# Retuned rules for which product TensorE takes next in a fused adaLN + attention + mixer-MLP kernel

## The chip, the cores and the metric

The kernel runs on one core of one Trainium2 chip. The metric is the device time of one execution in microseconds (us); the reported value is the median of three runs. TensorE (PE in the profile, with its weight loads as PEld), VectorE (DVE), ScalarE (ACT), GpSimd (POOL) and SyncE (SP, which issues the DMAs) run side by side and meet at semaphores.

## The reference

`x` is 2048 x 512. Six modulation rows come from `silu(c) @ w_mod`. Then, with layer norms that are scaled and shifted by these rows:

```python
h = _layernorm(x) * (1 + ca) + sa
x = x + ga * attention(h, wqkv, wo)              # 32 heads of 16
h = _layernorm(x) * (1 + cb) + sb
# mixer block B
g  = _gelu(_layernorm(h) @ w1)                   # its 4 column groups shifted by +1, -1, +2, -2 rows
x1 = h + shifted(g) @ w2
x  = x + gb * (x1 + _gelu(_layernorm(x1) @ w3) @ w4)   # 512 -> 1792 -> 512
```

In the attention each head forms `softmax(q k^T / 4) v` over 2048 keys.

## The kernel before, in words

**Work.** Heads are taken in pairs (16 pairs) and queries in four chunks of 512: 64 units. A unit has 16 key tiles of 128 keys. For each key tile and head TensorE makes one score product `sc` (line 1036, 64 rows of the array, 512 columns). ScalarE turns it into exponentials (line 1032), stored as 32-bit words. The upper 16 bits of each word are used as they are; GpSimd scales the lower 16 bits (`p_low`, line 1087), or ScalarE does it in two halves when GpSimd is far behind. To know the row maxima beforehand TensorE also makes, 24 key tiles ahead (`LEAD`), the maximum product `mb` (line 1020), and VectorE reduces it (line 1016). One `mb` for one head and one `sc` for the other use the two halves of the array at the same time; the text calls the two a *row pair*. There are 2048 `mb` and 2048 `sc`. The *P·V products* `pv` come in groups of four that share the array by columns: a group with the upper halves of one key tile (line 1113), a group with the lower halves of two key tiles (line 1110), the *late* one. All else is *other products*: the q, k and v projections, wo, w1 to w4 (each as three products of split factors, lines 355, 357 and 359; `w1` to `w4` and `wo` read their weights from the tile `wr`), and transposes (`ot`, `xT`, `tr`).

**PSUM.** Seven banks are shared by `mb`, `sc` and the other products, which may hold up to three; the eighth holds `pv`. A row pair needs two free banks: one that VectorE has reduced and one that ScalarE has read.

**Order.** Nothing is decided on the chip. A planner in Python (`Sched` and the loop at the end of the kernel function) writes the instructions in one fixed order, with a clock of its own for each engine. It calls a run of products of one kind a *lump* and remembers the kind in `mode`: `"r"` (rows), `"c"` (P·V), `"o"` (other). `Sched.to` adds `SWITCH` to TensorE's planned clock at each change of kind and `ENTER` besides where the new kind is not P·V.

In each turn the loop finds `nc_`, the number of P·V groups that are ready (at most `CMOST` = 6), and `slack`, the time until the banks and the reading engine would let a lump of `GRP` = 3 row pairs run without a wait. Inside a lump of fewer than three pairs a next pair is called if its wait is at most `STAY`. From another kind a row lump is called when `slack` is at most `BACK` = 150 ns, unless there is so much *credit* (owed time of other products, filled at each row by `budget`) that it passes `CHIGH`. If no row is called, P·V runs when `CMIN` = 4 groups are ready (or fewer that fit into the slack); else other products run, while the clock is below `now + slack + GRACE` and credit is above zero, or above `-OVER` while a product sits half done in its bank (`sch.open`). If none of these ran, a row is called once its first pair has banks.

Of the kernel before, what the change touches and what calls it, by code (L numbers as in the profile page):

```python
# [50 lines left out]
OVER = 3000.0  # L51
CROW, CCOL, CIN, CMID, COUT = 232.0, 230.0, 105.0, 95.0, 95.0
# [28 lines left out]
VP = 2  # L81
UWAIT = 4
XB = 4
SWITCH, ENTER = 95.0, 107.0
EARLY, STAY, BACK, GRACE = 300.0, 300.0, 150.0, 0.0
OWE, CTOP, OMIN = 1500.0, 7000.0, 0.0
CHIGH, CMIN, CMOST, PTLOW, PLAG = 6500.0, 4, 6, 2, 1


class Sched:  # L90

# [235 lines left out]
def kernel(ctx, tc, A_x, A_wqkv, A_wo, B_w1, B_w2, B_w3, B_w4, c, w_mod, out):  # L327
# [83 lines left out]
    sch = Sched()  # L411
# [509 lines left out]
    def drain(flag):  # L921
        while flag not in done:
            sch.step()
# [50 lines left out]
    pts = [at.tile([P, 2, CH], I32, name=f"pt{i}") for i in range(NPT)]  # L974
# [97 lines left out]
    def p_low(s):  # L1072

        p = pt[s].rearrange("p j n -> p (j n)")
        o, i = p.bitcast(F16)[:, 0::2], p.bitcast(U16)[:, 0::2]
        ready = e_exp.pop(s) + XX
        g, a = [max(sch.T[e], ready) for e in "GA"]
        if g > a + LACT:

            def half(h):  # L1080
                c = slice(h * CH, (h + 1) * CH)
                e_low[s] = XP["A"] + sch.crit("A", 690, ready, partial(act.activation, o[:, c], i[:, c], AF.Copy, scale=0.5))
            half(0)
            e_low[s] += 690 + 480
            second.append(partial(half, 1))
        else:
            e_low[s] = XP["G"] + sch.crit("G", 1345, ready, lambda: pool.tensor_scalar(  # L1087
                o, i, 0.5, 1.0, op0=OP.mult, op1=OP.mult))
# [38 lines left out]
    def ac_copy():  # L1127
        u, e = acs.pop()
        if u:
            drain(("of", u - 1))  # L1130
        ac = at.tile([P, CH], F32, name="ac", tag="ac", bufs=1)
        acc = pv.pop(u)
        e = sch.crit("A", cA(), e + PX, lambda: act.activation(ac, acc, AF.Copy))
        v_free[0] = e + XP["A"]
        sch.add(o_fin(u, ac, e + XP["A"]), 0)
# [439 lines left out]
    def budget(s):  # L1575
        if s < 0:
            return 800.0
        return min(BTOP, max([BLOW] + [(1000.0 * w - sch.spent) / (d - s) for d, w in DUES if d > s]))
# [5 lines left out]
    def before(s):  # L1584

        nu, r = divmod(s + 32, 16)
        if r == 0 and 0 < nu < NU:
            asked.append(nu)
        if asked:
            ci, pr = units[asked[0]]  # L1590
            keys = [("kq", pr // 4)] + [("q", pr // 8)] * (ci > 0)
            if r >= UWAIT:
                for key in keys:
                    drain(key)
            if all(key in done for key in keys):
                load_unit(asked.pop())
        if s in VAT:
            i = VAT.index(s)
            for kt in range(4 * i, 4 * i + 4):
                while kt not in near and ("vk", 0, kt) not in done:  # L1600
                    sch.step()
                if kt not in near:
                    sch.dma(dma.dma_start, vst[i][:, kt % 4], Vs[0, :, kt])
        if s == NS - 12:
            done.add("keys")
        if s == -12:
            unit_tiles(at, 2, dve, pool)
# [18 lines left out]
    def cols():  # L1626
        n, t = 0, sch.T["P"] + (sch.mode != "c") * SWITCH
        for y in pvs[:CMOST]:
            if n and y[0] % NKT == 0 and not y[1]:
                break  # L1630
            if col_at(y) > t + 20:
                break
            t += CCOL
            n += 1
        return n

    def fillers():
        for e in "ADG":
            sch.misc(e, max(sch.T["P"], sch.T[e]) + TOLE[e])

    def do_cols(n):
        sch.to("c")
        for y in pvs[:n]:
            if not y[1]:
                e_hi.pop(y[0])
            pv_part(*y)
        del pvs[:n]

    def do_row(x, t):
        sch.T["P"] = t  # L1650
        sch.to("r")
        late = sorted(e_exp)
        one_row(x)
        for q in late:
            if 2 * q < x - 2 * PLAG:
                p_low(q)
# [3 lines left out]
    while x < end or pvs or acs:  # L1660
        if acs:
            ac_copy()
        can = x < end
        if can:
            s, i = divmod(x, 2)
            if x == LENDS:
                sch.most = MOST
            if i == 0 and seen != s:
                seen = s
                before(s)  # L1670
                if s >= 0 and s % 16 == 0:
                    drain(("shift", s // 16))
            can = i or s < 0 or bool(pts)
        now, row, slack = sch.T["P"], False, LATE
        if can:
            need = (s >= 0) + (s + LEAD < NS)
            sch.flush(need)
            free = sorted(sm.t)
            one = free[need - 1 + 2 * (s < 0)]
            if one >= LATE:  # L1680
                one = free[need - 1]
            enter = (sch.mode != "r") * (SWITCH + ENTER)
        else:
            for q in sorted(e_exp):
                p_low(q)
            while second:
                second.pop(0)()
        nc_ = cols()
        if can:
            if sch.mode == "r" and burst < GRP:  # L1690
                slack = one - now
                row = slack <= STAY
            else:
                st = one
                for k in range(2, GRP + 1):
                    if need * k <= len(free) and free[need * k - 1] < LATE:
                        st = max(st, free[need * k - 1] - (k - 1) * CROW)
                dry = sch.T["D"] if s + LEAD < NS else sch.T["A"]
                slack = max(st, dry - CROW - PX - EARLY) - enter - now
                row = slack <= BACK and (sch.mode == "r" or sch.credit < CHIGH and not (nc_ >= CMIN and len(pts) <= PTLOW))  # L1700
        if not row:
            n = 0
            if nc_ >= CMIN or nc_ and slack >= nc_ * CCOL + (sch.mode != "c") * SWITCH:
                do_cols(nc_)
                n = nc_
            elif slack >= OMIN or sch.mode == "o" or sch.credit > CHIGH:
                stop = now + max(slack, 0.0) + GRACE
                while (sch.T["P"] < stop or sch.credit > CHIGH) and sch.credit > (-OVER if sch.open else 0.0) and sch.one():
                    n += 1
            if not n:  # L1710
                if not can or one - enter > now + 100.0:
                    sch.T["P"] = now + 50.0
                else:
                    row = True
        if row:
            do_row(x, max(now, one - enter))
            burst = 1 if enter else burst + 1
            x += 1
            sch.credit = max(min(sch.credit + budget(s) / 2, CTOP), -OWE)
        fillers()  # L1720
        if tp[0] is None and x >= 2 * (NS // NC + TPO) and (x >= 2 * (NS // NC + TPL) or all(key in done for key in KEYS)):
            for key in KEYS:
                drain(key)
            qpx.close()
            tpx = ExitStack()
            tp[0] = tpx.enter_context(tc.tile_pool(name="tp", bufs=1, side="right"))
# [43 lines left out]
```

## Time and profile before

| what | value |
|---|---|
| median of 3 runs | 2010.18 us (2007.87 to 2010.95) |
| the profiled execution's own time | 2012.32 us |
| its span, first to last instruction | 2010.5 us |
| granted TensorE clock, mean | 0.99 |
| instructions | 42313 |
| HBM read, written | 225.81 MB, 62.91 MB |

The profile was taken from one execution whose own time is 2.1 us above the median. A timeline row gives the start, the length, the engine, the line, the operation with the tile written and the tiles read, the shapes and a count. Matmuls are pipelined, so the length of one (0.39 to 0.5 us) says less than the distance between two starts, and the text goes by starts.

### The profile page before, as it was taken

The numbers are of one execution on the slowest core, as the hardware profiler recorded it, in microseconds if no ns is written. First come the engines' busy times: TensorE is split into PE (matmuls) and PEld (weight loads), VectorE is DVE, ScalarE is ACT, GpSimd is POOL, SyncE is SP. The second block draws the span as 40 slices with busy tenths as digits, with TensorE's granted clock in tenths as the row PEclk, the third lists the DMA queues.
The fourth block names the chain that finished last, engine by engine and source line by source line (L and its number), as shares of the span: only waits on it lengthen the run. The fifth ranks groups of instructions, "written<-read, shape, count | busy, mean of one in ns | idle before, by whom it ended". The sixth has DMA issues, their size and how long they took to land.

```text
span 2010.5 us, 42313 instructions
## 1 busy us (share of the span) xinstructions
PE 1960.9 (98%) x14480; PEld 1131.9 (56%) x14480; DVE 1681.5 (84%) x3010; ACT 1483.1 (74%) x3087; POOL 1672.8 (83%) x1598
## 2 busy tenths in 40 slices
PE   6999999999999999999999999999999999999899
PEld 4655565555445555555455555555555655555798
DVE  7978878888988898888999889888988888883643
ACT  5377798878878777777887877787787877777343
POOL 6378889999988898888899989898899989887532
PEclk8999999999999999999999999999999999999999
DMA  5677588776533333335333334333433343333432
GB/s 184 195 208 232 170 247 274 229 250 212 200 97 105 114 114 126 122 109 166 104 105 114 105 111 126 126 113 110 156 110 96 118 135 114 114 94 128 158 149 90
DMA packets 233083, 293.24 MB, mean 146 GB/s; under 512 B 125876, under 2 KB 178052, under 8 KB 216580
## 3 DMA queue, kind: packets, MB, share of 16 engines
q1 hardware_dynamic: 232868, 290.53, 45.4%
q8 instruction: 115, 1.88, 0.4%
q14 instruction: 100, 0.82, 0.1%
HBM read 225.81 MB, written 62.91 MB: 144 GB/s over the span
## 4 chain that ended last, share of the span: by engine, by line
PE 79%; DVE 10%; ACT 4%; DMA 2%; POOL 2%; issue 1%; SPq 1%; POOLq 0%; ACTq 0%; DVEq 0%
PE mb L1020 15%; PE sc L1036 13%; PE pv L1113 11%; PE w L355 8%; PE w L357 8%; PE w L359 7%; PE pv L1110 7%; DVE mx L1016 6%; ACT pt L1032 2%; PE ot L1145 1%; POOL pt L1087 1%; PE xT L1223 1%; PE v L355 1%; PE mr L660 1%; PE v L359 1%
## 5 line engine op out<-in xcount | busy, mean ns | idle before, releaser
L1016 DVE TENSOR_REDUCE mx<-mb 128x1 f32<-128x512 f32 x2048 | 1296.5, 683 | 139.8 <-PE mb L1020 112.8
L1087 POOL TENSOR_SCALAR pt<-pt 128x1024 f16<-128x1024 uint16 x977 | 1301.2, 1366 | 103.7 <-ACT pt L1032 99.9
L1032 ACT ACTIVATE pt<-sc 128x512 int32<-128x512 f32 x2048 | 1100.1, 602 | 313.6 <-PE mb L1020 238.5
L1020 PE MATMUL mb<-kst,qtl 64*128 64x512 f32 x2048 | 732.5, 449 | 15.2 <-DVE mx L1016 4.1
L1036 PE MATMUL sc<-qtl,kst 64*128 64x512 f32 x2048 | 705.7, 441 | 4.4 <-DVE mx L1016 2.2
L1020 PEld LDWEIGHTS mb<-kst,qtl 64*128 64x128 f32 x2048 | 342.8, 193 | 183.1 <-DVE mx L1016 80.2
L1036 PEld LDWEIGHTS sc<-qtl,kst 64*128 64x128 f32 x2048 | 333.4, 185 | 129.3 <-issue 45.7
L1113 PE MATMUL pv<-pt,vst 128*32 128x512 f16 x4096 | 359.0, 394 | 2.2 <-DMA vst<-Vs 2.1
L1110 PE MATMUL pv<-pt,vst 128*17 128x512 f16 (+1 forms) x2048 | 213.8, 399 | 0.5 <-POOL pt L1087 0.3
L1447 POOL TENSOR_TENSOR g<-xs,g 128x256 fp32r<-128x256 f32 (+2 forms) x144 | 103.4, 719 | 96.1 <-ACT g L1446 92.4
L1113 PEld LDWEIGHTS <-vst 128*32 128x32 bf16 x4096 | 114.4, 94 | 119.2 <-issue 69.9
L355 PE MATMUL w<-A,wr 128*128 128x256 f32 (+2 forms) x576 | 174.9, 304 | 0.7 <-ACT A L349 0.5
L357 PE MATMUL w<-A,wr 128*128 128x256 f32 (+2 forms) x576 | 172.9, 300 | 0.5 <-DVE A L345 0.3
L359 PE MATMUL w<-A,wr 128*128 128x256 f32 (+2 forms) x576 | 172.9, 300 | 0.0
L1110 PEld LDWEIGHTS <-vst 128*17 128x17 f16 (+1 forms) x2048 | 54.0, 90 | 139.5 <-issue 130.1
L355 PEld LDWEIGHTS w<-A,wr 128*128 128x128 f32 x576 | 110.3, 191 | 28.1 <-issue 19.5
L357 PEld LDWEIGHTS w<-A,wr 128*128 128x128 f32 x576 | 110.1, 191 | 24.6 <-issue 23.3
L359 PEld LDWEIGHTS w<-A,wr 128*128 128x128 f32 x576 | 110.1, 191 | 24.4 <-issue 24.4
L355 PE MATMUL w<-wr,g 128*128 128x512 f32 x288 | 122.6, 426 | 0.6 <-ACT g L1446 0.6
L357 PE MATMUL w<-wr,g 128*128 128x512 f32 x288 | 119.5, 415 | 0.0
L359 PE MATMUL w<-wr,g 128*128 128x512 f32 x288 | 119.2, 414 | 0.2 <-POOL g L1447 0.2
L1437 DVE SCALAR_TENSOR_TENSOR sq<-sq,w 128x256 f32<-128x256 f32 (+2 forms) x144 | 60.4, 420 | 47.0 <-ACT sq L1443 44.2
(150 smaller groups left out, 2099.4 us busy)
## 6 DMA issues: line engine op xcount, KB each, us to landing
wr<-Ws SPq DMA_DIRECT2D x80, 1024.0 KB
kst<-Ks SPq DMA_DIRECT2D x189, 256.0 KB
vst<-Vs SPq DMA_DIRECT2D x252, 192.0 KB
qtl<-Qs SPq DMA_DIRECT2D x192, 64.0 KB
Vs<-vt SPq DMA_DIRECT2D x32, 384.0 KB
Ws<-wq SPq DMA_DIRECT2D x40, 256.0 KB
Ws<-wst SPq DMA_DIRECT2D x40, 256.0 KB
wst<-in_B_w_dram SPq DMA_DIRECT2D x36, 256.0 KB
```

The source lines that it names most:

```text
L355: te.matmul(o, lh, rh, start=first, stop=False)
L357: te.matmul(o, lh, rl, start=False, stop=False)
L359: te.matmul(o, ll, rh, start=False, stop=last)
L1016: end = sch.crit("D", 605, e + PX, lambda: dve.reduce_max(mxs[u][:, j, g, c:c + 1], b, axis=AX.X))
L1020: return ready, lambda: te.matmul(b, lhs, kst[u % 3][r, c * CH:(c + 1) * CH], start=True, stop=True), after
L1032: ea = sch.crit("A", 480, e + PX, lambda: act.activation(pt[s][:, j], b, AF.Exp))
L1036: return ready, lambda: te.matmul(b, kst[u % 3][r, kt * P:(kt + 1) * P], qst[u][r], start=True, stop=True), after
L1087: e_low[s] = XP["G"] + sch.crit("G", 1345, ready, lambda: pool.tensor_scalar(o, i, 0.5, 1.0, op0=OP.mult, op1=OP.mult))
L1110: te.matmul(acc[r:r + n, :], v[:, (kt + i) % 4, c - n:c].bitcast(F16), pt[s + i].bitcast(F16)[:, j, 0::2], start=False, stop=kt == NKT - 2 ...
L1113: te.matmul(acc[r:r + 32, :], v[:, kt % 4, r:r + 32], pt[s].bitcast(F16)[:, j, 1::2], start=kt == 0, stop=False, skip_group_check=True)
L1437: dve.scalar_tensor_tensor(sq, sq, 1.0 / GELU_A, b, op0=OP.add, op1=OP.mult)
L1447: ("G", cG(n), lambda: pool.tensor_tensor(lo, xs, hi, op=OP.subtract)), (None, 0, end), bank=b)
```

## The change

It changes numbers of the planner and two of its conditions. `SWITCH` becomes 105. `STAY` becomes 200, `GRACE` 400, `CHIGH` 9000, `PTLOW` 3, `OVER` 1500. When P·V is the present kind, other products are begun only if the slack is at least `OMINC` = 800 ns. After rows, with credit above `OFIRST` = 1500 and more than `PTLOW` free buffers of exponentials, ready P·V groups are passed over for other products, unless they fit into the slack. No instruction's form changes.

```diff
-SWITCH, ENTER = 95.0, 107.0
+SWITCH, ENTER = 105.0, 107.0
 EARLY, STAY, BACK, GRACE = 300.0, 300.0, 150.0, 0.0
-OWE, CTOP, OMIN = 1500.0, 7000.0, 0.0
+OWE, CTOP, OMIN, OMINC, OFIRST = 1500.0, 7000.0, 0.0, 800.0, 1500.0
 CHIGH, CMIN, CMOST, PTLOW, PLAG = 6500.0, 4, 6, 2, 1
+CHIGH = 9000.0
+STAY = 200.0
+GRACE = 400.0
+PTLOW = 3
+OVER = 1500.0
...
         if not row:
             n = 0
-            if nc_ >= CMIN or nc_ and slack >= nc_ * CCOL + (sch.mode != "c") * SWITCH:
+            if nc_ >= CMIN and not (sch.mode == "r" and sch.credit > OFIRST and len(pts) > PTLOW) or nc_ and slack >= nc_ * CCOL + (sch.mode != "c") * SWITCH:
                 do_cols(nc_)
                 n = nc_
-            elif slack >= OMIN or sch.mode == "o" or sch.credit > CHIGH:
+            elif slack >= (OMINC if sch.mode == "c" else OMIN) or sch.mode == "o" or sch.credit > CHIGH:
                 stop = now + max(slack, 0.0) + GRACE
                 while (sch.T["P"] < stop or sch.credit > CHIGH) and sch.credit > (-OVER if sch.open else 0.0) and sch.one():
                     n += 1
```

The order of TensorE's products in the whole program, counted in lumps (both programs have the same 14392 matmul instructions, 4096 of rows, 6144 of P·V and 4152 of others):

| | before | now |
|---|---|---|
| row lumps | 731 | 827 |
| P·V lumps | 636 | 516 |
| lumps of other products | 635 | 449 |
| changes of kind | 2001 | 1791 |
| P·V to rows / P·V to other | 146 / 490 | 458 / 58 |
| rows to P·V / rows to other | 587 / 144 | 437 / 390 |
| other to rows / other to P·V | 585 / 49 | 369 / 79 |
| row lumps straight after P·V, of 1 / 2 / 3 pairs | 8 / 20 / 94 | 59 / 194 / 179 |
| row lumps after other products, of 1 / 2 / 3 pairs | 4 / 91 / 463 | 3 / 91 / 254 |
| matmuls after the last row product | 828 | 911 |

(The two rows on sizes are for the stretch in which all three kinds alternate, 136 to 1850 us in the profile of before.) Two places show the pattern. The first is on TensorE in the middle of the third query chunk, about the 1495th row pair: w4 products (written to `w`) between row pairs. Before, from the end of one P·V lump to the start of the next:

```order
L1113 MATMUL pv<-pt_618,vst_612 32x512
L355 MATMUL w_20505<-wr,g_19563 128x512
L357 MATMUL w_20505<-wr,g_19563 128x512
L359 MATMUL w_20505<-wr,g_19563 128x512
L1036 MATMUL sc<-qtl_151,kst_153 128x512
L1020 MATMUL mb<-kst_789,qtl_787 128x512 x2
L1036 MATMUL sc<-qtl_151,kst_153 128x512
L1036 MATMUL sc<-qtl_605,kst_607 128x512
L1020 MATMUL mb<-kst_789,qtl_787 128x512
L1110 LDWEIGHTS vst_612
```

And now, at the same P·V group on TensorE:

```order
L1119 MATMUL pv<-pt_618,vst_612 32x512
L1042 MATMUL sc<-qtl_605,kst_607 128x512
L1026 MATMUL mb<-kst_801,qtl_799 128x512 x2
L1042 MATMUL sc<-qtl_605,kst_607 128x512
L365 MATMUL w_20403<-wr,g_19772 128x512
L361 MATMUL w_20403<-wr,g_19772 128x512
L363 MATMUL w_20403<-wr,g_19772 128x512
L1042 MATMUL sc<-qtl_605,kst_607 128x512
L1026 MATMUL mb<-kst_801,qtl_799 128x512 x2
L1042 MATMUL sc<-qtl_605,kst_607 128x512 x2
L1026 MATMUL mb<-kst_801,qtl_799 128x512
L1116 LDWEIGHTS vst_612
```

The three w4 products stood between P·V and rows; now two row pairs stand between P·V and them, and three more pairs behind them. (All lines of the new file from there on are 6 higher.) The second place is on TensorE where the attention output of a unit is transposed (`ot`), some 15 row pairs later. Before, from the end of a P·V lump:

```order
L1113 MATMUL pv<-pt_616,vst_609 32x512
L1145 MATMUL ot<-ident,ac 128x128 x4
L355 MATMUL w_20652<-wr,g_19951 128x512
L357 MATMUL w_20652<-wr,g_19951 128x512
L359 MATMUL w_20652<-wr,g_19951 128x512
L355 MATMUL w_20652<-wr,g_19951 128x512
L1036 MATMUL sc<-qtl_605,kst_607 128x512
L1020 MATMUL mb<-kst_789,qtl_787 128x512 x2
```

Now:

```order
L1119 MATMUL pv<-pt_616,vst_609 32x512
L1026 MATMUL mb<-kst_801,qtl_799 128x512
L1042 MATMUL sc<-qtl_605,kst_607 128x512 x2
L1026 MATMUL mb<-kst_801,qtl_799 128x512
L365 MATMUL w_20403<-wr,g_19772 128x512
L1151 MATMUL ot<-ident,ac 128x128 x4
L361 MATMUL w_20671<-wr,g_19772 128x512
L363 MATMUL w_20671<-wr,g_19772 128x512
L365 MATMUL w_20671<-wr,g_19772 128x512
```

Again two row pairs moved ahead of the other products, and the lump of other products is longer (ten products against eight).

## The prediction

> **What bounds the kernel now.** I read the page first, then the busy time by stage, then the starts on TensorE.
>
> ```profile
> span 2010.5 us, 42313 instructions
> ...
> PE 1960.9 (98%) x14480; PEld 1131.9 (56%) x14480; DVE 1681.5 (84%) x3010; ACT 1483.1 (74%) x3087; POOL 1672.8 (83%) x1598
> ...
> PE 79%; DVE 10%; ACT 4%; DMA 2%; POOL 2%; issue 1%; SPq 1%; POOLq 0%; ACTq 0%; DVEq 0%
> ```
>
> ```profile
> 0.00:136.00 136.00, 117.23 (x640) 78.68 (x640) 106.97 (x192) 69.93 (x142) 72.52 (x88) 0.95 0.63 195
> 136.00:700.00 564.00, 552.03 (x4154) 301.43 (x4153) 494.88 (x859) 456.12 (x934) 513.34 (x463) 0.98 0.62 195
> 700.00:1850.00 1150.00, 1141.31 (x8866) 621.01 (x8864) 1000.86 (x1799) 896.18 (x1881) 1024.08 (x961) 1.00 0.37 118
> 1850.00:2010.50 160.50, 150.32 (x828) 130.80 (x824) 78.83 (x163) 60.88 (x136) 62.84 (x89) 0.97 0.37 133
> ```
>
> The second fence has, for the start, two stretches of attention and the end, the length and then the busy time of PE, PEld, DVE, ACT and POOL, the granted clock and the DMA share. TensorE is the bound: 98% busy, and 79% of the chain of waits that ended last. But a busy TensorE is not one that streams. Here is one whole cycle of lumps, with nothing late:
>
> ```profile
> 1510.14 0.50 PE L1036 MATMUL sc<-qtl,kst 64*128 64x512 f32 x1
> 1510.15 0.73 PE L1020 MATMUL mb<-kst,qtl 64*128 64x512 f32 x2
> 1510.49 0.62 PE L1036 MATMUL sc<-qtl,kst 64*128 64x512 f32 x2
> 1510.72 0.39 PE L1020 MATMUL mb<-kst,qtl 64*128 64x512 f32 x1
> 1511.04 0.41 PE L1110 MATMUL pv<-pt,vst 128*17 128x512 f16 x4
> 1511.28 0.41 PE L1113 MATMUL pv<-pt,vst 128*32 128x512 f16 x4
> 1511.62 0.39 PE L355 MATMUL w<-A,wr 128*128 128x256 f32 x1
> 1511.85 0.28 PE L357 MATMUL w<-A,wr 128*128 128x256 f32 x1
> 1511.96 0.27 PE L359 MATMUL w<-A,wr 128*128 128x256 f32 x1
> 1512.08 0.28 PE L355 MATMUL w<-A,wr 128*128 128x256 f32 x1
> 1512.28 0.51 PE L1020 MATMUL mb<-kst,qtl 64*128 64x512 f32 x1
> ```
>
> Read the starts. Second to third row pair: 1510.49 to 1510.72, 0.23 us, the pace of a row pair. First to second: 0.35, so the first step of a row lump costs 0.11 more. Last pair to P·V: 0.32, so the change costs 0.09. One P·V group to the next: 0.24, with hardly a first-step price; P·V to another product: 0.34, 0.11 above the pace. Among 256-wide products 0.11 to 0.12 is the pace; the first step takes 0.23 (0.11 more) and the change to rows 0.20 (0.09 more). Over all steps the distances repeat so closely that medians can be used: 340 ns and 233 ns for the first and later steps in rows (689 and 610 of them), 337 and 231 for 512-wide other products, 223 and 118 for 256-wide ones, 341 from P·V to rows against 225 between P·V groups, 326 from rows or a 512-wide product to another kind. Hence three prices: 107 ns for the first step of a row or other lump, 115 ns for a change out of P·V, 95 ns for any other change.
>
> **The change part by part.** No product is added or removed, so only the order costs or gains.
>
> *Changes.* Out of P·V: 490 + 146 = 636 before, 58 + 458 = 516 now, 120 fewer at 0.115 = 13.8 us. All others: 1365 before, 1275 now, 90 fewer at 0.095 = 8.5 us. Together -22.3 us.
>
> *First steps.* Row lumps 731 to 827 (+96), lumps of other products 635 to 449 (-186): 90 fewer at 0.107 = -9.6 us. TensorE's own work so falls by 31.9 us. All of it lies on the path, since TensorE is it.
>
> *Waits for row banks.* This is where the gain can be lost. The row lumps that follow P·V straight grow from 146 to 458, and such lumps wait more. First and last of 93 three-pair row lumps straight after P·V (136 to 1810 us):
>
> ```profile
> 139.74 0.50 PE L1036 MATMUL sc<-qtl,kst 64*128 64x512 f32 x1
> 140.09 0.61 PE L1036 MATMUL sc<-qtl,kst 64*128 64x512 f32 x2
> 140.33 0.43 PE L1020 MATMUL mb<-kst,qtl 64*128 64x512 f32 x1
> ...
> 1805.61 0.49 PE L1036 MATMUL sc<-qtl,kst 64*128 64x512 f32 x1
> 1806.25 0.81 PE L1036 MATMUL sc<-qtl,kst 64*128 64x512 f32 x2
> 1806.85 0.50 PE L1020 MATMUL mb<-kst,qtl 64*128 64x512 f32 x1
> ```
>
> First and last of 447 after other products:
>
> ```profile
> 137.70 0.50 PE L1020 MATMUL mb<-kst,qtl 64*128 64x512 f32 x1
> 138.04 0.96 PE L1020 MATMUL mb<-kst,qtl 64*128 64x512 f32 x2
> 138.49 0.50 PE L1036 MATMUL sc<-qtl,kst 64*128 64x512 f32 x1
> ...
> 1809.35 0.50 PE L1020 MATMUL mb<-kst,qtl 64*128 64x512 f32 x1
> 1809.69 0.74 PE L1020 MATMUL mb<-kst,qtl 64*128 64x512 f32 x2
> 1809.94 0.50 PE L1036 MATMUL sc<-qtl,kst 64*128 64x512 f32 x1
> ```
>
> From first to third pair the four take 0.59, 1.24, 0.79 and 0.59 us; without a wait it is 0.34 + 0.23 = 0.57. The mean over the 93 is 0.765 us, a wait of 194 ns; over the 447 it is 0.609, a wait of 38 ns. A two-pair lump has one of the two inner steps; I give it half, 97 and 19 ns. By these means the row lumps before (20 of two and 94 of three pairs after P·V, 91 and 463 after others) wait 1.9 + 18.2 + 1.7 + 17.6 = 39.4 us, and now (194 and 179, 91 and 254) 18.8 + 34.7 + 1.7 + 9.7 = 64.9: +25 us. That is the upper end. The lower end comes from `STAY`: a pair that would wait over 200 ns now ends the lump. If each inner wait of before is cut at 200 ns, the means fall to 113 and 51 ns (three and two pairs, after P·V) and 19 and 11 ns, and the sum now is 20.2 + 9.9 + 4.8 + 1.0 = 35.9 us: -4. What these waits are for is seen at the weight loads, where the semaphores stand:
>
> ```profile
> PEld mb L1020 <- DVE mx L1016: 80.2, 231, 1.2
> ...
> PEld mb L1020 <- ACT pt L1032: 29.2, 80, 1.0
> ```
>
> It is VectorE's reduction above all. Its pace is in this row of three: (1.89 - 0.68) / 2 = 0.605 us for each `mb`.
>
> ```profile
> 1804.90 1.89 DVE L1016 TENSOR_REDUCE mx<-mb 128x1 f32<-128x512 f32 x3 [0.22 <-PE mb L1020]
> 1806.71 0.68 DVE L1554 TENSOR_TENSOR x<-x,w 128x512 f32<-128x512 f32 x1
> ```
>
> The cycle of before at the first place of the change, priced by the rows at 1510.14 (with a P·V lump of three groups and four 256-wide products): 0.90 for rows, 0.81 for P·V, 0.66 for others, 2.37 us, in which VectorE reduces three pairs, 1.82 us; it has 0.55 us for its other work. The cycle now has two more pairs (0.35 + 0.32 = 0.67): 3.04 us against 5 x 0.605 = 3.03 us. VectorE has nothing left there and falls behind until a longer lump of other products comes. So I take the wait term from the upper half of its range, +14 us. The Trainium skill, TensorEngine Tiling (Array Packing), section PSUM Bottleneck, says that packing speeds up TensorE but not the emptying of PSUM, so that the copy out may become the bound; by that rule the term would stand at its upper end or beyond (the second rival). The 84% of VectorE's row do not bear it out over the span, the lumps after P·V do in part.
>
> *P·V after rows* falls from 587 to 437, others after rows rise from 144 to 390. The first waits for exponentials and for `p_low`, the second only for a bank; I set the difference at nothing. P·V is passed over for others only while more than three buffers of exponentials are free; behind it nothing queues but ScalarE's next exponentials, and with that cover gone a row pair would wait for a buffer.
>
> *The end.* After the last row product stand 83 more matmuls, some 12 us by the paces above. They leave the middle, which gets as much shorter; in the last stretch TensorE is busy 150 of 160 us, so they cost what they cost elsewhere.
>
> *Other engines.* `p_low` runs 980 times on GpSimd instead of 977, and 88 halves instead of 94 on ScalarE: a few us on engines that are 83% and 74% busy. SyncE issues the same loads in another order; DMA share in the long stretch is 0.37. Nothing.
>
> *Sum.* -22.3 - 9.6 + 14 = -17.9 us against the profiled execution's own 2012.3 us: 1994.4. The median of the runs lies 2.1 us lower, so 1992 us. A change within 0.2% (4 us) can't be told from none.
>
> **The rivals.**
>
> 1. *The waits do not grow.* With 200 ns as the longest wait inside a lump and longer lumps of other products, VectorE is always ahead when rows begin. For it: the row lumps of before already wait only 38 ns after other products. Against it: the 194 ns after P·V. Wait term -4: 2010.2 - 31.9 - 4 = 1974 us.
> 2. *VectorE sets the pace, and it is slower than before.* The place is the cycle of five pairs above. If each of the 59 + 194 short row lumps after P·V marks a cycle in which TensorE waits the 0.2 us that `STAY` allows, that is 51 us; 2010.2 - 31.9 + 51 = 2029 us. It decides from 31.9 / 253 = 0.126 us for each. For it: the even count of 3.04 against 3.03 us. Against it: VectorE's 1000.9 busy us of 1150 in the long stretch, which leaves 149 us to catch up in.
> 3. *The change moves the waits and nothing else.* The wait term is at its upper end, +25, and the P·V lumps after the two-pair lumps come before their exponentials by a few us: 2010.2 - 31.9 + 25 + 4 = 2007 us, no change.
> 4. *GpSimd binds the first stretch.* It is busy 513 of 564 us there; a stretch shortened by a third of 18 us would still be 558. It costs less than 5 us and stays inside my forecast.
>
> **How the numbers follow.** Forecast 55%, its own range 1980 to 2005 (wait term +2 to +27). First rival 20%, second 14%, third 11%. Faster by over 0.2% are the forecast and the first rival, 75%; same is the third, 11%; slower the second, 14%. The range takes in most of the first rival and the third: 1970 to 2014.
>
> **What would show it.** Right: TensorE's first-step and change distances stay at 107, 115 and 95 ns; the idle of `mb` and `sc` weight loads put down to VectorE grows, by tens of us; VectorE, with the same 3010 instructions, is a little busier as a share (1681 of some 1992, 84.4%); the time after the last row product grows by some 12 us. Wrong: three-pair lumps after P·V take 0.9 us and more from first to third pair (second rival), or 0.6 (first rival). The prediction falls if the waits per lump are not those of before, since its largest uncertain term assumes that a kind of lump keeps its wait when it becomes three times as frequent.

## The result, and the profile after

The changed kernel takes 1996.37 us (median of 4 runs, 1993.19 to 1998.32) against 2009.85 us before (4 runs, 2007.87 to 2010.95). The ratio is 0.9932, interval 0.9915 to 0.995: faster by 13.5 us, where 18 were forecast. The page of the changed kernel, its span, busy times and chain of waits by engine:

```profile
span 1991.4 us, 42269 instructions
...
PE 1933.8 (97%) x14480; PEld 1137.1 (57%) x14480; DVE 1669.9 (84%) x3010; ACT 1483.2 (74%) x3081; POOL 1671.0 (84%) x1601
...
PE 69%; DVE 9%; POOL 6%; ACT 6%; DMA 2%; issue 2%; SPq 1%; POOLq 0%; ACTq 0%; DVEq 0%
```

TensorE is busy 27 us less with the same 14480 matmuls; the others do what they did. Its share of the chain falls from 79% to 69%, and POOL and ACT gain: TensorE is still the bound, but it is released more often by somebody else. A cycle of the new pattern, on TensorE (start, length, then as before):

```profile
1344.73 0.50 PE L1026 MATMUL mb<-kst,qtl 64*128 64x512 f32 x1
...
1345.07 0.38 PE L1026 MATMUL mb<-kst,qtl 64*128 64x512 f32 x1
1345.30 0.40 PE L1042 MATMUL sc<-qtl,kst 64*128 64x512 f32 x1
...
1345.64 0.41 PE L1116 MATMUL pv<-pt,vst 128*17 128x512 f16 x4
1345.87 0.64 PE L1119 MATMUL pv<-pt,vst 128*32 128x512 f16 x8
1346.43 0.50 PE L1042 MATMUL sc<-qtl,kst 64*128 64x512 f32 x1
1346.44 0.73 PE L1026 MATMUL mb<-kst,qtl 64*128 64x512 f32 x2
1346.82 0.46 PE L1042 MATMUL sc<-qtl,kst 64*128 64x512 f32 x1
1347.21 0.50 PE L365 MATMUL w<-wr,g 128*128 128x512 f32 x1
1347.55 0.40 PE L361 MATMUL w<-wr,g 128*128 128x512 f32 x1
1347.78 0.40 PE L363 MATMUL w<-wr,g 128*128 128x512 f32 x1
1348.11 0.49 PE L1042 MATMUL sc<-qtl,kst 64*128 64x512 f32 x1
```

and VectorE beside it:

```profile
1343.87 4.48 DVE L1022 TENSOR_REDUCE mx<-mb 128x1 f32<-128x512 f32 x7
```

The prices stand where they stood: 0.34 and 0.23 us in the first lump, 0.34 to P·V, 0.23 between groups, 0.34 and 0.23 among 512-wide products, 0.33 back to rows. The cycle with its five row pairs takes 3.38 us, and VectorE reduces seven banks in one piece of 4.48 us: it has no idle moment in this cycle, as counted beforehand. TensorE loses 0.1 us at the end of the second row lump: the `sc` of its second pair comes at 1346.82 instead of 1346.77, and the w4 product 0.39 us later instead of 0.33. The load of that `sc` stands in the timeline without a wait that somebody ended, so this delay can't be put down to VectorE:

```profile
1346.79 0.18 PEld L1042 LDWEIGHTS sc<-qtl,kst 64*128 64x128 f32 x1
```

What the place does show is that a row product's delay can appear *behind* the lump, at the change to the next kind, when it is the last pair's second product that came late. A wait has a second price, too. Where the last pair of a lump came on time and with both its products together, the next kind starts 329 ns (P·V, 307 times) or 331 ns (other products, 220 times) behind it, by the medians of the changed kernel; where that pair, still together, had waited 40 ns or more, it is 434 (48 times) and 435 ns (21 times). The kernel before has 329 and 434 for P·V as well. So a wait costs its length and then 0.105 us more, about the price of a first step, one step later.

To divide the whole span, I priced every distance between two starts on TensorE by its kind (the 35th percentile of that kind over all profiles of this study) and called the rest a wait. Own work so follows the counts by construction; what the profiles add is that the distances themselves stayed, the medians of the main kinds within 2 ns from the kernel before to the changed one. First to last start, in us:

| | before | changed | difference |
|---|---|---|---|
| own work, priced | 1841.6 | 1812.4 | -29.2 |
| waits up to the 64th row pair | 25.4 | 33.1 | +7.7 |
| into and inside row lumps, later | 58.4 | 54.8 | -3.6 |
| rows to other products | 6.9 | 23.5 | +16.6 |
| rows to P·V | 36.2 | 30.4 | -5.8 |
| all other places of the middle | 19.5 | 16.2 | -3.3 |
| after the last row product | 13.1 | 11.8 | -1.3 |
| first to last start | 2001.2 | 1982.1 | -19.1 |

(Rows are rounded, so a column may miss its sum by 0.1. With the median of each kind in place of the 35th percentile the two differences are -25 and +6 us instead of -29.2 and +10.2, so the split is good to some 4 us.) The profiled execution of the changed kernel was the fastest of its four, 1993.19 us, so that the profiles differ by 19.1 us and the medians by 13.5. The +7.7 us of the start hold two new waits of P·V groups that the new order makes too early, by the timeline of the changed kernel:

```profile
102.32 0.41 PE L1119 MATMUL pv<-pt,vst 128*32 128x512 f16 x4 [2.67 <-DMA vst<-Vs]
...
133.11 0.40 PE L1116 MATMUL pv<-pt,vst 128*25 128x512 f16 x3 [3.10 <-POOL pt L1093]
```

One waits for a V tile's load, the other for GpSimd's `p_low`.

### The profile page after: what moved, and what is told of

It is laid out like the page before. It is cut to its first block, busy times and chain, and to the rows that moved or that the text cites. A ratio compares the mean times of both kernels' runs of the same rounds, so it can differ in the third digit from the quotient of the medians.

```text
span 1991.4 us, 42269 instructions
## 1 busy us (share of the span) xinstructions
PE 1933.8 (97%) x14480; PEld 1137.1 (57%) x14480; DVE 1669.9 (84%) x3010; ACT 1483.2 (74%) x3081; POOL 1671.0 (84%) x1601
## 3 DMA queue, kind: packets, MB, share of 16 engines
q1 hardware_dynamic: 232868, 290.53, 45.8%
## 4 chain that ended last, share of the span: by engine, by line
PE 69%; DVE 9%; POOL 6%; ACT 6%; DMA 2%; issue 2%; SPq 1%; POOLq 0%; ACTq 0%; DVEq 0%
PE mb L1026 14%; PE sc L1042 11%; PE pv L1119 10%; PE w L361 7%; PE w L363 7%; PE w L365 7%; PE pv L1116 6%; DVE mx L1022 6%; POOL pt L1093 4%; ACT pt L1038 3%; PE ot L1151 1%; SPq L125 1%; DMA wr<-Ws 1%; PE q L365 1%; PE q L361 1%
## 5 line engine op out<-in xcount | busy, mean ns | idle before, releaser
L1026 PE MATMUL mb<-kst,qtl 64*128 64x512 f32 x2048 | 754.0, 455 | 18.3 <-DVE mx L1022 7.0
L1042 PE MATMUL sc<-qtl,kst 64*128 64x512 f32 x2048 | 728.3, 445 | 1.6 <-ACT pt L1038 0.7
L1026 PEld LDWEIGHTS mb<-kst,qtl 64*128 64x128 f32 x2048 | 347.1, 192 | 228.6 <-DVE mx L1022 108.4
L1042 PEld LDWEIGHTS sc<-qtl,kst 64*128 64x128 f32 x2048 | 334.9, 185 | 155.9 <-issue 52.5
L1119 PE MATMUL pv<-pt,vst 128*32 128x512 f16 x4096 | 348.8, 392 | 5.5 <-DMA vst<-Vs 4.9
L361 PE MATMUL w<-A,wr 128*128 128x256 f32 (+2 forms) x576 | 172.0, 299 | 0.6 <-ACT A L355 0.3
L363 PE MATMUL w<-A,wr 128*128 128x256 f32 (+2 forms) x576 | 170.0, 295 | 0.5 <-DVE A L351 0.3
L365 PE MATMUL w<-A,wr 128*128 128x256 f32 (+2 forms) x576 | 169.2, 294 | 0.0
L361 PE MATMUL w<-wr,g 128*128 128x512 f32 x288 | 119.9, 416 | 0.8 <-ACT g L1452 0.6
L365 PE MATMUL w<-wr,g 128*128 128x512 f32 x288 | 118.1, 410 | 0.2 <-POOL g L1453 0.2
L363 PE MATMUL w<-wr,g 128*128 128x512 f32 x288 | 117.5, 408 | 0.0
L1449 ACT ACTIVATE sq<-w 128x256 f32<-128x256 f32 (+2 forms) x144 | 55.8, 388 | 66.8 <-PE w L365 65.3
```

The lines of the kernel that those rows point to most:

```text
L361: te.matmul(o, lh, rh, start=first, stop=False)
L363: te.matmul(o, lh, rl, start=False, stop=False)
L365: te.matmul(o, ll, rh, start=False, stop=last)
L1026: return ready, lambda: te.matmul(b, lhs, kst[u % 3][r, c * CH:(c + 1) * CH], start=True, stop=True), after
L1042: return ready, lambda: te.matmul(b, kst[u % 3][r, kt * P:(kt + 1) * P], qst[u][r], start=True, stop=True), after
L1119: te.matmul(acc[r:r + 32, :], v[:, kt % 4, r:r + 32], pt[s].bitcast(F16)[:, j, 1::2], start=kt == 0, stop=False, skip_group_check=True)
```

## Experiments

Theory A: the prices of changes and first steps decide, and a lump keeps the wait of its kind. Theory B: VectorE's draining of the row banks sets the pace, and waits take what changes give. Own work and waits are from the same division; ratios are against the kernel before as timed beside each group of kernels (medians 2009.85 to 2010.57 us).

| kernel | own work | waits | median us | ratio, interval |
|---|---|---|---|---|
| before | 1841.6 | 159.5 | 2009.85 | |
| changed | 1812.4 | 169.7 | 1996.37 | 0.9932, 0.9915 to 0.995 |
| conditions alone | 1838.9 | 161.3 | 2012.57 | 1.0012, 1.0003 to 1.0021 |
| OMINC 0 | 1824.8 | 187.4 | 2021.28 | 1.0055, 1.0043 to 1.0067 |
| CHIGH 6500 | 1824.3 | 183.7 | 2018.7 | 1.0044, 1.003 to 1.0058 |
| STAY 150 | 1822.8 | 171.4 | 2005.17 | 0.9975, 0.9966 to 0.9985 |
| STAY 300 | 1796.4 | 197.6 | 2007.19 | 0.9987, 0.9979 to 0.9996 |
| STAY 400 | 1766.6 | 275.1 | 2048.9 | 1.0192, 1.0178 to 1.0206 |
| GRACE 0 | 1820.2 | 172.8 | 2007.02 | 0.9985, 0.9975 to 0.9995 |
| OFIRST off | 1812.0 | 175.8 | 1997.31 | 0.9936, 0.9923 to 0.995 |
| OMINC 1200 | 1813.1 | 178.3 | 2002.73 | 0.9969, 0.9958 to 0.998 |
| changed, half maximum | 1812.4 | 142.7 | 1965.97 | 0.9785, 0.9772 to 0.9797 |
| STAY 400, half maximum | 1766.6 | 225.6 | 2003.85 | 0.9965, 0.9952 to 0.9978 |

**STAY back at 300, and 400.**

```diff
-STAY = 200.0
+STAY = 300.0      # and 400.0 in the next
```

> The changed kernel with STAY at its old 300 ns, all else as changed. Counted in its order: 1712 changes of kind (1791 in the changed kernel), 787 row lumps and 394 of other products (827 and 449). Priced at 115, 95 and 107 ns that is 17 us less of TensorE's own work than the changed kernel. Theory A (prices of changes and first steps decide, a row lump's wait stays near that of its kind): 4 to 12 us faster than the changed kernel, 18 to 26 us faster than the kernel before. Theory B (VectorE's draining of banks sets the pace, so waits take what changes give): within 4 us of the changed kernel or slower than it, with inner waits of three-pair lumps after P·V back near 190 ns.

> The changed kernel with STAY at 400 ns. Counted: 1569 changes, 727 row lumps, 303 of other products; priced, 47 us less of TensorE's own work than the changed kernel, and 412 three-pair lumps straight after P·V instead of 179. Theory A: 15 to 30 us faster than the changed kernel. Theory B: within 6 us of the changed kernel, or slower, the row waits grown by 40 us or more.

With 300 the own work fell by 16.0 us, as priced, and the waits rose by 27.9: 10.8 us slower than the changed kernel by the medians. With 400, own work -45.8 and waits +105.4: 52.5 us slower. Theory A is refuted for the waits: a lump's wait does not stay that of its kind. B gave the sign, but its prediction of where failed: three-pair lumps after P·V wait 86 ns inside with 300, not 190 (237 of them), and 170 ns with 400 (399 of them). The rest stands in the other lumps, at the lumps' starts and at the change to P·V (30.4 us in the changed kernel, 37.9 with 300). The weight loads' idle, by what ended it, STAY 400:

```profile
PEld mb L1026 <- DVE mx L1022: 154.1, 406, 4.5
```

and the changed kernel:

```profile
PEld mb L1026 <- DVE mx L1022: 108.4, 299, 1.9
...
PEld sc L1042 <- ACT pt L1038: 37.1, 104, 0.7
PEld mb L1026 <- ACT pt L1038: 35.4, 94, 0.9
```

The first number is the total in us, the second the count: VectorE releases 406 of the waiting loads instead of 299. With 300, though, the row does not follow the waits; it is below that of the changed kernel:

```profile
PEld mb L1026 <- DVE mx L1022: 95.9, 267, 1.1
```

The chain of waits that ended last points to VectorE more evenly: its share is 9% in the changed kernel, 12% with 300 and 20% with 400. The chain of STAY 400:

```profile
PE 63%; DVE 20%; ACT 7%; DMA 3%; issue 2%; POOL 2%; SPq 2%; POOLq 0%; ACTq 0%; DVEq 0%
```

**VectorE's drain made shorter, order unchanged.** The maximum is taken over half of each bank; q is scaled down so that the exponentials stay finite. What the kernel computes is changed by both.

```diff
-dve.reduce_max(mxs[u][:, j, g, c:c + 1], b, axis=AX.X)
+dve.reduce_max(mxs[u][:, j, g, c:c + 1], b[:, :256], axis=AX.X)
-sch.chain(*split_ops(*t, b, 0.25), qk_store
+sch.chain(*split_ops(*t, b, 0.0025), qk_store
```

> The changed kernel with VectorE's maximum taken over 256 of the 512 columns of each bank, and q scaled by 0.0025 instead of 0.25 so that the exponentials stay finite without the true maximum; the order of all instructions is that of the changed kernel. VectorE then drains a bank in some 0.34 us instead of 0.605. Theory B (the row waits are VectorE's draining): 25 to 60 us faster than the changed kernel, the weight loads' idle put down to the reduction down to a third. A rival that the waits come from exponentials or from times the planner misjudges: less than 15 us faster.

> The kernel with STAY 400 and the same half maximum, order unchanged against that one. It has 46 us less of TensorE's own work than the changed kernel and 106 us more of waits. Theory B: the waits fall to about those of the changed kernel with the half maximum, so this kernel becomes the faster of the two by 20 to 45 us, near 1920 us. Rival (misjudged times, exponentials): it stays slower than the changed kernel with the half maximum.

In the order of the changed kernel the time fell by 30.4 us, the waits by 27.0. The groups and the weight loads' idle of that run:

```profile
L1022 DVE TENSOR_REDUCE mx<-mb 128x1 f32<-128x256 f32 x2048 | 768.1, 418 | 447.0 <-PE mb L1026 333.8
```

```profile
PEld mb L1026 <- DVE mx L1022: 57.1, 149, 0.8
...
PEld sc L1042 <- ACT pt L1038: 44.1, 125, 0.7
PEld mb L1026 <- ACT pt L1038: 43.9, 114, 1.0
```

A reduction takes 418 ns instead of 682 (from start to start of two that follow each other without a gap 0.33 to 0.34 us instead of 0.60), and the loads it releases wait 57.1 us instead of 108.4 (half, not the third expected); those that ScalarE releases wait more. The waits from rows to other products fall from 23.5 to 11.1 us, rows to P·V from 30.4 to 20.9, into and inside row lumps from 54.8 to 47.2. Together that is 29.5 of 108.7 us, so VectorE's drain has a part in all three, the largest in the first. At least 27 of the 170 us of waits hang on it: a reduction shortened by 39%, not taken away, gives twice the gain of the change.

In the order of STAY 400 the time fell by 45 us, but the kernel stays 38 us slower than the changed one with the same reduction, where B expected it to be the faster. Of its 105 us of additional waits 83 remain when VectorE's work is cut (225.6 against 142.7). Its loads:

```profile
PEld sc L1042 <- issue: 80.4, 189, 11.2
PEld sc L1042 <- ACT pt L1038: 59.6, 206, 0.8
...
PEld mb L1026 <- DVE mx L1022: 55.2, 131, 2.8
```

ScalarE's exponentials now release 206 waiting `sc` loads (125 in the order of the changed kernel). They drain the other bank of each pair, and one after the other without a gap they start 0.48 us apart with either reduction. So once a reduction takes 0.34 us, ScalarE is the slower of the two drains. B in its narrow form is refuted too: the row waits are not VectorE's alone. And 15 of the 83 us are no row banks at all, but two waits of TensorE for DMA loads; STAY 400 with the full reduction has both (10.6 and 4.1 us), the changed kernel neither:

```profile
PE sc L1042 <- DMA qtl<-nm: 10.9, 1, 10.9
...
PE w L361 <- DMA wr<-Ws: 4.0, 1, 4.0
```

What share the planner puts there itself, by calling pairs that are up to 400 ns from ready, was not separated from this.

**The conditions.**

```diff
-OWE, CTOP, OMIN, OMINC, OFIRST = 1500.0, 7000.0, 0.0, 800.0, 1500.0
+OWE, CTOP, OMIN, OMINC, OFIRST = 1500.0, 7000.0, 0.0, 0.0, 1500.0     # OMINC 0; 1200 in another
+                                                           800.0, 1e9  # OFIRST off
```

> The changed kernel with OMINC 0, so that after P·V other products may begin at any slack, as before. Counted: 1884 changes, 624 of them out of P·V; priced, 9 us more of TensorE's own work than the changed kernel. Theory A: 5 to 12 us slower than the changed kernel, that is 2 to 9 us faster than the kernel before. Theory B: no slower than the changed kernel, since 245 row lumps after P·V instead of 458 wait less.

> The kernel before with the two new conditions alone (OMINC 800 and OFIRST 1500), all numbers old. Counted: 1986 changes and 1359 first steps against 2001 and 1366 of before; priced, 2.4 us less. Theory A: within 4 us of the kernel before, since the conditions move little without the numbers. A rival that the conditions are the core of the change: 10 us faster or more.

> The changed kernel with OMINC 1200 instead of 800. Counted: 1791 changes, 1275 first steps against 1276; 500 instead of 458 row lumps straight after P·V; priced, the same own work within 3 us. Theory C: 8 to 20 us slower than the changed kernel. Theory D: within 4 us of it, since what OMINC does is done at 800 already.

> The changed kernel without OFIRST (ready P·V groups are never passed over after rows). Counted: 1790 changes, 828 row lumps, 437 of other products (1791, 827, 449); priced, the same own work of TensorE within 1 us, the same kinds of lumps, but another order in detail. Theory C (the changed kernel's low waits are a property of its one order, and any reshuffle of the same kinds of lumps loses it): 8 to 20 us slower than the changed kernel. Theory D (the rules set the waits): within 4 us of it.

OMINC 0 is 24.9 us slower than the changed kernel: own work +12.4 (9 priced) and waits +17.7 where both theories saw none or fewer. With 245 instead of 458 row lumps after P·V the row lumps wait *more*: into and inside 66.1 us against 54.8. So it is not the closeness of rows to P·V alone that makes waits. A likely reason is that with OMINC 800 other products follow rows (390 changes, 155 here) and stand between two row lumps that P·V would leave too close; no run tests this by itself. By itself, in the numbers of before, the condition does little: the two conditions alone give own work -2.7 and a time within 4 us of before, as A expected. OMINC 1200 loses 6.4 us at equal own work, between the two expectations. OFIRST does nothing (1997.31 against 1996.37 us), though the order differs in detail throughout. That refutes theory C, that the low waits are luck of one order, for a reshuffle that keeps the kinds of lumps.

**CHIGH, GRACE, STAY 150.**

```diff
-CHIGH = 9000.0
+CHIGH = 6500.0
-GRACE = 400.0     # another kernel
+GRACE = 0.0
-STAY = 200.0      # another kernel
+STAY = 150.0
```

> The changed kernel with CHIGH at its old 6500. Counted: 1864 changes, 571 of them out of P·V, 1294 first steps; priced, 10 us more of TensorE's own work than the changed kernel. If prices alone decide: 8 to 12 us slower than the changed kernel. If waits shrink as TensorE's own work grows: within 4 us of it.

> The changed kernel with GRACE 0. Counted: 1845 changes, 844 row lumps, 470 of other products; priced, 9 us more own work than the changed kernel (0.115 x 16 + 0.095 x 38 + 0.107 x 38). Theory D: 4 to 10 us slower than the changed kernel, with waits no larger, since VectorE is no longer left waiting by lumps that run on. Theory C: 15 to 30 us slower, own work and waits both up.

> The changed kernel with STAY 150. Counted: 1851 changes, 847 row lumps, 467 of other products; priced, 11 us more own work than the changed kernel. Theory D: the waits go on falling from 300 over 200 to 150 ns, so 0 to 8 us slower than the changed kernel. Theory C: waits 10 to 25 us up as well, 18 us slower or more.

CHIGH 6500 costs 22.3 us: own work +11.9 (10 priced) and waits +14.0, which neither expectation had. GRACE 0 costs 10.7 us, 7.8 of them own work (9 priced), waits +3.1; STAY 150 costs 8.8 us, own work +10.4 (11 priced), waits +1.7. Both lie just past the upper end of theory D, for own work as priced; their waits did not fall as D had it, but they did not rise by C's 10 us and more either. Why the waits of CHIGH rise is open. Of the four values of STAY that were timed 200 is the best: at 150 there are more changes and first steps and no fewer waits, above 200 waits cost more than changes and first steps save. Below 150 nothing is known; a kernel with STAY 100 gave no time. `SWITCH`, `PTLOW` and `OVER` were not tried alone.

No kernel here is faster than the changed one at full work.

## Why the prediction was right

The sum was right in size (-17.9 forecast; -19.1 in the profiles, -13.5 in the medians), but not every term of it, and that it came out is in part luck: the row waits were put 17.6 us too high, and waits at two places that stood at nothing or not at all came to +18.5.

- *Changes and first steps*, -22.3 and -9.6: -29.2 measured. The three prices stayed: by medians 341 and 234 ns for the first and later steps in rows (340 and 233 before), 337 and 232 for 512-wide products, 223 and 119 for 256-wide ones, 343 from P·V to rows (341 before). With them own work followed the priced counts within 4 us in every kernel whose counts were priced beforehand. This is the firm part.
- *Waits for row banks*, range -4 to +25, taken at +14: -3.6 measured into and inside row lumps. The step that failed is the one behind the +14, that a kind of lump keeps its wait when it becomes three times as frequent; the prediction itself named this as the thing on which it falls. Three-pair lumps after P·V take 0.648 us from first to third pair (170 of them), not 0.765, a wait of 77 ns instead of 194; two-pair lumps after P·V wait 20 ns, not the 97 assumed. The lower end was right, for the reason given there (`STAY` ends a lump before the long wait), and so was the first rival's term of -4.
- *P·V after rows and others after rows*, set at nothing: -5.8 and +16.6 us measured, +10.8 together. This is the mis-sized term, and most of it is a matter of counts. After the 64th row pair a change from rows to other products waits 55 ns on average before (125 of them) and 63 now (371); one to P·V waits 63 (581) and 71 (429). At the old means the new counts alone give +13.6 and -9.5 us. About half of the larger one hangs on VectorE's drain, since the half maximum takes it from 23.5 to 11.1 us. So part of the price of a cycle in which VectorE has nothing left came out in the term beside the one I gave it to.
- *The start* was not in the sum; two P·V groups called too early cost 6 us of +7.7.
- *The end*: own work after the last row product grew from 143.6 to 153.4 us, forecast 12.
- The signs: the loads' idle for VectorE grew from 80.2 to 108.4 us, and VectorE's share stayed at 84%, both as forecast. The first of them was no good sign of TensorE's own waits, which fell by 3.6 us in the row lumps.
- The first rival (waits do not grow) had the row lumps right (its sign was 0.6 us for three pairs after P·V, and 0.648 is nearer to that than to 0.765), but its 1974 us did not come, because of the waits at the start and at the changes from rows. The second (VectorE slower than before) and the third (no change) did not come. STAY 400 comes nearest to the second, with 399 three-pair lumps after P·V and 39 us more than before, but with the half maximum 38 us of its loss against the changed kernel remain, so VectorE is not the whole of it. The Trainium skill, TensorEngine Tiling (Array Packing), section PSUM Bottleneck, says that tiling makes TensorE faster but not the emptying of PSUM, which may become the bottleneck (it speaks of a fourfold speedup; the row pairs here are two products at a time). In the order of STAY 400 the trace agrees in part: VectorE's share of the chain is 20%, and the shorter reduction gives back 45 us.

## What to carry to other kernels

Where one engine is busy all the time by the profile, count its changes of kind and first steps and price each by the distance of starts; such a sum held to a few us in every order here. Waits did not add up that way: with three engines 74 to 84% busy behind TensorE's banks, some of what was taken from its own work came back as waits, and a mean wait per kind of lump did not carry over to another order. The best setting is where the two slopes meet, so try a wait limit on both sides. Look for a bank's wait at the step behind the lump as well as inside it, and count 0.105 us more for each.

## What the runs showed that was not expected

- The trade of own work against waits is far from even: from STAY 150 to 200 own work falls by 10.4 us and waits by 1.7; from 200 to 300 own work falls by 16.0 and waits rise by 27.9; from 300 to 400 it is 29.8 against 77.5.
- The same order with a reduction of 418 instead of 682 ns runs 30.4 us faster, though VectorE was 84% busy and on 9% of the chain only.
- Returning one of OMINC, CHIGH, STAY and GRACE to its old value loses 10.7 to 24.9 us, where the whole change gains 13.5; the conditions without the numbers gain nothing.
